# A transformer block's backward pass on one core: where the gate row is multiplied in, and which queues carry the last stores and loads

## The chip, the cores and the metric

The kernel runs on one core of a Trainium2 chip. A core has a matrix engine (TensorE, PE in the profile), an elementwise engine (VectorE, DVE), an activation engine (ScalarE, ACT), a general engine (GpSimd, POOL) and a synchronisation engine (SyncE, SP). Each runs its own list of instructions strictly in order and waits on semaphores for the others. Here SyncE, GpSimd and, in a few places, ScalarE also issue the transfers between the chip's memory and the core's on-chip memory. The metric is the device time of one execution in microseconds (us), lower is better.

## The reference, cut to what matters

The program computes the output of one block and all gradients of it.

```python
def _A_ref(x, w_r, w_i):                       # spectral filter over sequence and channels
    X = rfft2(x.astype(float32)) * (w_r + 1j * w_i)
    return irfft2(X, s=(S, D)).astype(bfloat16)
def _B_ref(x, w1, b1, w2, b2):                 # feed-forward with squared relu
    r = relu(x @ w1 + b1)
    return (r * r) @ w2 + b2
mod = (silu(c) @ w_mod)                        # six rows: sa, ca, ga, sb, cb, gb
h = layernorm(x) * (1 + ca) + sa
x = x + ga * _A_ref(h, A_w_r, A_w_i)
h = layernorm(x) * (1 + cb) + sb
x = x + gb * _B_ref(h, w1, b1, w2, b2)
```

S is 2048, D is 512, the hidden size F is 1792, everything in bf16. The gradients asked for are those of x, w_r, w_i, w1, b1, w2, b2, c and w_mod. Two matter here. With g the incoming gradient and h = r*r the hidden rows, w2's gradient is the product of h transposed with (g * gb), and b2's is the column sum of g * gb. Since gb is one row, the same for every token, it can be multiplied into the product after it is formed or into g before.

## The kernel before

The 2048 rows are held as 16 tiles t of 128 partitions by 512 channels (`NT` = 16). Instructions are traced by a Python program in one order, and a scheduler then places them in each engine's list by priority and by which data and buffers are free; `tc.issue_after(ins)` makes what the block traces come behind `ins` on that engine, and `high_priority` moves an instruction forward. Buffers come from pools with a fixed number of slots per name; a new pool may lie over the memory of a released one, and its first writers then wait for the last users there, stores included.

The program runs forward and backward through the feed-forward part up to about 285 us. What follows is the part that the diff touches.

*The filter phase* (`spec_f23` with `ew_b` and `after_b`, eight groups gi). TensorE transforms a group into PSUM, ScalarE copies it to `G`, VectorE multiplies it with the filter (giving `Z`) and with the saved spectrum (giving the filter's gradient `gW`, three buffers). Each `gW` is stored to out_2 and out_3 by four transfers of 64.2 KB (six of them for gi = 0) on SyncE's queue (L1170). Units of w1's gradient (`grad_w1`, L1126: 16 matmuls, a ScalarE copy, and after every second unit a store on GpSimd's queue) fill TensorE between groups. The modulation gradients (`gm.emit`, with tiles `wmc`, `gmbc`, `gwm` in the pool `gmp`) are put between groups too. At gi = 4 the first two tiles `hn` of the transposed hidden rows are loaded (`load_hn`, a transposing transfer of 512 KB on SyncE's queue); at gi = 5 `gmp` is released and g is loaded whole, 2 MB, into `g_sb` in its place.

*The G1 phase* (`spec_g1`, eight groups). TensorE multiplies `Z` into PSUM (`psG`, four buffers); VectorE (L351) and ScalarE (L353) copy alternate halves to `CS`. Every later `psT` needs the whole of `CS`.

*The row phase* works on eight pairs of tiles. For each pair: TensorE forms `psT` (L375), ScalarE copies it to `Tsb` (L377), TensorE forms `psY` (L385), ScalarE copies it to `gs` (L1276). VectorE unfolds it to `gh1` (L266 to L270) and multiplies by a row, giving `gn` (L1278); ScalarE scales it and sums it (L1280); VectorE multiplies `gh1` with the loaded rows `n1` (`q1`, L1281) and sums a product (`jk1`, L1285), scales the two sums (L1287), applies them to `n1` (L1289, one instruction for each tile of the pair), adds (L1290), adds the loaded `gxl` (L1292), and SyncE stores the result (L1293). `load_rows3(t + 4)` then loads `n1` and `gxl` for the pair after next, from a pool `fin` with two buffers. TensorE also adds up columns (`colsums1`, L1262), two pairs behind.

Between the pairs `fill` puts units of w2's gradient, 14 in all: `grad_w2(fc)` is 16 matmuls of `hn` with `g_sb` (L1203) into one of two PSUM buffers `mm`, then one instruction that takes it out, and the store (L1207):

```python
        with tc.high_priority():
            nc.vector.tensor_tensor(gw, ps, modb[:, GB_B, :], op=ALU.mult)
        nc.sync.dma_start(out6_view[:, fc, :], gw)
        load_hn()
```

`modb[:, GB_B, :]` is the gate row gb on all partitions. `hn` has two buffers in `hnp`, two in `gwp` and four in `endp`; the last pool exists once the w1 units are done. `grad_b2` sums g's columns on TensorE and multiplies the row by gb at the end (`add_quadrants` with `scale`, L1107). The last two modulation gradients (j = 0 and 1, L456 to L477) and the last units of w2's gradient close the program.

Of the kernel before, what the change touches and what calls it, by code (L numbers as in the profile page):

```python
# [18 lines left out]
D = 512  # L19
DF = 257  # L20
# [314 lines left out]

def spec_g1(tc, K, Z, CS):
    nc = tc.nc
    with tc.tile_pool(name="psG", bufs=4, space=PSUM) as psG_pool, tc.tile_pool(name="psF", bufs=1, space=PSUM) as psF_pool:
        psF = psF_pool.tile([P, 4, P], FP32, name="psF")
        for gi in range(8):  # L340
            for hh in range(2):
                n = 2 * gi + hh
                ps = psG_pool.tile([P, 2, 2 * P], FP32, name="psG")
                for ch in range(2):
                    for ri in range(2):
                        nc.tensor.matmul(ps[:, ch, :], lhsT=Z[gi][:, hh, ri, ch:256:2],  # L346
                                         rhs=K["LG"][:, n, ri:ri + 2, :].rearrange("p y m -> p (y m)"), start=(ri == 0), stop=(ri == 1))
# [96 lines left out]
class GMod:  # L444
# [12 lines left out]

    def emit(self, jc, q, row, pool, ppool):

# [21 lines left out]
def kernel(  # L481
# [586 lines left out]

    lf2 = tc.alloc_tile_pool(name="lf2", bufs=1, side="right")
    gmp = tc.alloc_tile_pool(name="gmp", bufs=1, side="right")  # L1070
    K["LF"] += [lf2.tile([P, 2, 3, P], BF16, name=f"LFb{gi}") for gi in range(4, 8)]
# [20 lines left out]

    def add_quadrants(ps, pool, out, scale=None):
        w = ps.shape[-1]
# [5 lines left out]
        def add():  # L1100
# [13 lines left out]
    def run_later(n=1):  # L1114
        if later:
            later[0][0] -= n
            if later[0][0] <= 0:
                later.pop(0)[1]()

    w1o = {}  # L1120
# [28 lines left out]
    with tc.tile_pool(name="f23b", bufs=2) as fr, tc.tile_pool(name="ewb", bufs=2) as ew:  # L1149
# [14 lines left out]
        def ew_b(gi, G):  # L1164
# [3 lines left out]
            for i, o in enumerate((out_2, out_3)):  # L1168
                for p0_, n, rows_ in w_parts(o, gi):
                    K["gW"] = nc.sync.dma_start(rows_, gW[p0_:p0_ + n, i, :, 0:DF]).ins  # L1170

        def after_b(gi):
            if gi + 4 < 8:
                load(gi + 4)
            if gi == 3:
                with tc.issue_after(K["gW"]):
                    nc.sync.dma_start(K["LG"], LG_dram)
            fill_w1(2 if 0 < gi < 6 else 1)
            if gi == 4:
# [9 lines left out]
            if gi in (0, 1, 3, 4):  # L1189
                gms.pop(0)[1]()  # L1190
                if len(gms) > 1:
                    gm.load(gms[1][0], gmp)
# [3 lines left out]
    fin = tc.alloc_tile_pool(name="fin", bufs=2, side="right")  # L1196
    gwp = tc.alloc_tile_pool(name="gwp", bufs=1, side="right")
    endp["gw"] = gwp

    def grad_w2(fc):  # L1200
# [4 lines left out]
        with tc.high_priority():  # L1205
            nc.vector.tensor_tensor(gw, ps, modb[:, GB_B, :], op=ALU.mult)  # L1206
        nc.sync.dma_start(out6_view[:, fc, :], gw)  # L1207
        load_hn()

    def grad_b2():  # L1210
        ps = psX.tile([P, D], FP32, name="mm")
        for t in range(NT):
            q = 32 * (t % 4)
            nc.tensor.matmul(ps[q:q + 32, :], lhsT=K["ones_q"], rhs=g_sb[:, t, :], start=(t < 4), stop=(t >= 12), tile_position=(0, q))
        add_quadrants(ps, gwp, out_7[None, :], modb[0:1, GB_B, :])

    rows3 = {}

    def load_rows3(t):
        if t < NT:  # L1220
            rows3[t] = (fin.tile([P, 2, D], BF16, name="n1"), fin.tile([P, 2, D], BF16, name="gxl"))
            nc.sync.dma_start(rows3[t][0], n1_dram[:, t:t + 2, :])
            nc.sync.dma_start(rows3[t][1], gx1_dram[:, t:t + 2, :])

    with tc.issue_after(K["g_load"]):
        load_rows3(0)
        load_rows3(2)
    for _ in range(2):
        load_hn()

    CS = utcs.tile([P, NT, 4, 16, 8], BF16, name="utcs")
    spec_g1(tc, K, Z, CS)
    sp.release()
    lg2.release()
    fp = tc.alloc_tile_pool(name="fin2", bufs=2, side="right")
    psX = tc.alloc_tile_pool(name="psX", bufs=1, space=PSUM)
    units2 = [lambda fc=fc: grad_w2(fc) for fc in range(NFC)]

    def fill(n):
        for _ in range(n):  # L1240
            if units:
                fill_w1(1)
                if not units:
                    gwa.release()
                    gap.release()
                    endp["hn"] = endp["gm"] = tc.alloc_tile_pool(name="endp", bufs=2)
                    endp["more"] = 4
            elif units2:
                units2.pop(0)()
                run_later()  # L1250
                if endp.get("more", 0) > 0:
                    endp["more"] -= 1
                    load_hn()

    with tc.tile_pool(name="psE", bufs=2, space=PSUM) as psE, tc.tile_pool(name="psS1", bufs=1, space=PSUM) as psS1:
# [11 lines left out]
        def row_pair(t, Ts):  # L1267
# [20 lines left out]
            for i in range(2):  # L1288
                nc.vector.tensor_scalar(gn[:, i, :], n1[:, i, :], rr[:, i, 3:4], rr[:, i, 2:3], op0=ALU.mult, op1=ALU.add)  # L1289
            nc.vector.tensor_tensor(gs, gn, gs, op=ALU.add)  # L1290
            gx = fp.tile([P, 2, D], BF16, name="gx")
            nc.vector.tensor_tensor(gx, gs, gxl, op=ALU.add)  # L1292
            nc.sync.dma_start(out1_view[:, t:t + 2, :], gx)  # L1293
            load_rows3(t + 4)

        Ts = g2_pair(0)
        for t in range(0, NT, 2):
# [4 lines left out]
            if t == 10:  # L1302
                grad_b2()
        fill(1)
        late.flush()
        acc1_odd = fp.tile([64, D], FP32, name="acc1_odd", bufs=1)
        nc.scalar.copy(out=acc1_odd, in_=acc1[64:128, :])
        acc1_sb = fp.tile([64, D], BF16, name="acc1_sb", bufs=1)
# [19 lines left out]
    fp.release()  # L1328
    gwp.release()
    fin.release()  # L1330
    endp["g"].release()
    lf2.release()
# [39 lines left out]
```

## Time and profile before

Six runs have a median of 429.61 us (428.13 to 430.58). The profiled execution took 429.44 us; its span, from the first instruction to the last, is 427.7 us, and 1.7 us lie around it.

| Stretch of the span | What runs | us |
|---|---|---|
| 287 to 338 | filter phase and w1's gradient | 51 |
| 338 to 347 | G1 phase | 9 |
| 347 to 356 | first rows, last w1 units | 9 |
| 356 to 412 | row phase with w2 units | 56 |
| 412 to 422.5 | last three w2 units | 10.5 |
| 422.5 to 427.7 | last stores and closing | 5 |

Some groups of that part, as the profile names them: mean ns of one instruction.

| Line | Engine | What | Count | Mean ns |
|---|---|---|---|---|
| L1203 | TensorE | w2 unit matmul, 128x512 | 224 | 388 |
| L1206 | VectorE | gw from PSUM times gb, 128x512 | 14 | 685 |
| L1289 | VectorE | sums applied to n1, 128x512 | 16 | 408 |
| L1290 | VectorE | add, 128x1024 | 8 | 684 |
| L1280 | ScalarE | scale and sum, 128x512 | 16 | 720 |
| L940 | ScalarE | Identity with scale and bias, 128x512 | 16 | 809 |
| L465 | ScalarE | copy from PSUM, 128x512 | 6 | 586 |
| L1170 | SyncE queue | gW store, 64.2 KB, to landing | 30 | 7600 |
| L477 | GpSimd queue | modulation gradient store, 256 KB, to landing | 12 | 6700 |

How to read this: a matmul's duration spans its way through the array, so matmuls that follow each other overlap; 48 of them in a row took 10.48 us, 0.218 us each. Instructions of the other engines overlap a little at their ends: two L1289 in a row took 0.73 us. "Idle before, released by" means that the engine stood still and which event ended it; a stretch's busy time over its length tells which engine is full there.

### The profile page before, as it was taken

The numbers are of one execution on the slowest core, as the hardware profiler recorded it, in microseconds if no ns is written. First come the engines' busy times: TensorE is split into PE (matmuls) and PEld (weight loads), VectorE is DVE, ScalarE is ACT, GpSimd is POOL, SyncE is SP. The second block draws the span as 40 slices with busy tenths as digits, with TensorE's granted clock in tenths as the row PEclk, the third lists the DMA queues.
The fourth block names the chain that finished last, engine by engine and source line by source line (L and its number), as shares of the span: only waits on it lengthen the run. The fifth ranks groups of instructions, "written<-read, shape, count | busy, mean of one in ns | idle before, by whom it ended". The sixth has DMA issues, their size and how long they took to land.

```text
span 427.7 us, 7138 instructions
## 1 busy us (share of the span) xinstructions
PE 398.3 (93%) x2375; PEld 195.6 (46%) x2375; DVE 354.5 (83%) x862; ACT 256.3 (60%) x487; POOL 55.0 (13%) x135
## 2 busy tenths in 40 slices
PE   2789999999899999999999999999999999898995
PEld 0344446654444444444444444455555654343332
DVE  6889868959996488978897998937997956999994
ACT  5578699778882188248634856464756464636331
POOL 7447940000000000000000000002221000000011
PEclk9999999999999999999999999999999999999899
DMA  8999899979497369768975998989899999999983
GB/s 237 243 258 282 239 275 300 315 236 184 147 357 234 121 94 334 208 171 158 320 176 168 181 315 271 277 200 316 270 275 298 191 234 194 211 296 276 248 237 112
DMA packets 144227, 101.11 MB, mean 236 GB/s; under 512 B 98969, under 2 KB 127518, under 8 KB 143806
## 3 DMA queue, kind: packets, MB, share of 16 engines
q1 hardware_dynamic: 141034, 93.03, 83.3%
q0 software_dynamic: 2592, 7.09, 5.4%
q10 hardware_dynamic: 564, 0.53, 0.4%
q8 instruction: 19, 0.31, 0.3%
q14 instruction: 18, 0.15, 0.1%
HBM read 35.44 MB, written 41.60 MB: 180 GB/s over the span
## 4 chain that ended last, share of the span: by engine, by line
PE 53%; DVE 21%; ACT 16%; issue 4%; DMA 2%; POOL 2%; SPq 0%; ACTq 0%; DVEq 0%
PE og L906 12%; PE mm L877 10%; PE mm L1126 10%; PE mm L712 5%; PE mm L1203 3%; PE psG L346 3%; ACT gab L717 2%; PE psC L311 2%; ACT AE L329 1%; DVE jk L1285 1%; ACT Xs L313 1%; ACT AE L330 1%; PE acc L774 1%; DVE l_st L817 1%; PE psB L323 1%
## 5 line engine op out<-in xcount | busy, mean ns | idle before, releaser
L712 PE MATMUL mm<-gT,w2T 128*128 128x512 bf16 x224 | 57.7, 383 | 3.1 <-ACT gab L717 3.1
L877 PE MATMUL mm<-h2T,w 128*128 128x512 bf16 x224 | 53.4, 379 | 1.3 <-ACT r L879 1.2
L1203 PE MATMUL mm<-g_sb,hn 128*128 128x512 bf16 x224 | 52.3, 388 | 2.0 <-DVE gw L1206 2.0
L906 PE MATMUL og<-w1T,gab 128*128 128x512 bf16 x224 | 50.9, 379 | 0.8 <-DVE o L971 0.8
L1126 PE MATMUL mm<-gab,h_sb 128*128 128x448 bf16 x256 | 50.7, 352 | 0.0
L906 PE MATMUL og<-w,h 128*128 128x512 bf16 x224 | 50.1, 379 | 0.0
L879 ACT ACTIVATE r<-mm,b1col 128x512 bf16<-128x512 f32 x56 | 37.0, 686 | 6.1 <-PE mm L877 3.3
L1203 PEld LDWEIGHTS <-hn 128*128 128x128 bf16 x224 | 21.6, 99 | 29.5 <-issue 7.0
L877 PEld LDWEIGHTS <-w 128*128 128x128 bf16 x224 | 21.1, 97 | 30.0 <-issue 8.3
L1126 PEld LDWEIGHTS <-h_sb 128*128 128x128 bf16 x256 | 24.6, 98 | 21.8 <-issue 0.6
L906 PEld LDWEIGHTS <-h 128*128 128x128 bf16 x224 | 21.8, 98 | 26.1 <-issue 1.0
L906 PEld LDWEIGHTS <-gab 128*128 128x128 bf16 x224 | 21.6, 98 | 25.9 <-issue 1.4
L712 PEld LDWEIGHTS <-w2T 128*128 128x128 bf16 x224 | 21.2, 98 | 22.6 <-issue 6.6
L1280 ACT ACTIVATE gs<-gn,inv 128x512 bf16<-128x512 bf16 x16 | 11.4, 715 | 24.5 <-DVE gn L1278 24.5
L919 ACT CAST G<-og 128x512 bf16<-128x512 f32 x16 | 9.2, 581 | 28.1 <-PE og L906 28.1
L295 POOL MEMSET AE<- 128x2 bf16 x4 | 0.3, 102 | 194.1 <-PE mm L877 194.1
L477 POOL DMA_DIRECT2D out_dram<-gwm x12 | 8.7, 730 | 117.4 <-DVE gx L1292 57.2
L881 DVE TENSOR_TENSOR h<-r 128x1024 bf16<-128x1024 bf16 x28 | 19.3, 689 | 4.8 <-ACT r L879 4.8
L717 ACT CAST gab<-mm 128x512 bf16<-128x512 f32 x36 | 21.4, 601 | 1.7 <-PE mm L712 1.5
L475 DVE SCALAR_TENSOR_TENSOR gm_junk<-wmc,onef,gmbc 128x512 bf16<-128x512 bf16 x24 | 18.0, 749 | 3.3 <-ACT gmbc L465 1.5
L715 DVE CAST gab<-mm 128x512 bf16<-128x512 f32 x20 | 13.8, 688 | 7.0 <-PE mm L712 6.7
L377 ACT ACTIVATE Tsb<-psT 128x512 bf16<-128x512 f32 x32 | 18.5, 607 | 1.5 <-PE psT L375 1.0
(290 smaller groups left out, 801.2 us busy)
## 6 DMA issues: line engine op xcount, KB each, us to landing
h_dram<-h SPq DMA_DIRECT2D x28, 256.0 KB, 3.2
gh_dram<-gab SPq DMA_DIRECT2D x28, 256.0 KB, 4.3
w<-in_B_w_dram SPq DMA_DIRECT2D x2, 1792.0 KB
wmc<-in_w_mod_dram SPq DMA_DIRECT2D x12, 256.0 KB, 4.7
out_dram<-gwm POOLq DMA_DIRECT2D x12, 256.0 KB, 6.7
wz_dram<-Z SPq DMA_DIRECT2D x8, 258.0 KB, 4.0
xs_dram<-Xs SPq DMA_DIRECT2D x8, 258.0 KB, 4.4
Z<-wz_dram SPq DMA_DIRECT2D x8, 258.0 KB, 5.7
```

The lines of the kernel that those rows point to most:

```text
L346: nc.tensor.matmul(ps[:, ch, :], lhsT=Z[gi][:, hh, ri, ch:256:2], rhs=K["LG"][:, n, ri:ri + 2, :].rearrange("p y m -> p (y m)"), start=(ri ...
L377: nc.scalar.activation(Tsb, ps, AF.Copy, scale=EF_S)
L475: nc.vector.scalar_tensor_tensor(out=junk, in0=wmc[:, i, :], scalar=K["onef"], in1=gmbc, op0=ALU.mult, op1=ALU.mult, accum_out=self.gsc[:, ...
L712: nc.tensor.matmul(ps, lhsT=w2T[:, dc, fc * P:(fc + 1) * P], rhs=gT[b][:, :, dc, :], start=(dc == 0), stop=(dc == 3))
L715: nc.vector.tensor_copy(out=gaT[b][:, fc, :], in_=ps)
L717: nc.scalar.copy(out=gaT[b][:, fc, :], in_=ps)
L877: nc.tensor.matmul(ps, lhsT=w1[:, dc, (fc + i) * P:(fc + i + 1) * P], rhs=h2T[b][:, :, dc, :], start=(dc == 0), stop=(dc == 3))
L879: nc.scalar.activation(r[:, i, :], ps, AF.Relu, bias=b1col[:, fc + i:fc + i + 1])
L881: nc.vector.tensor_tensor(h2, r, r, op=ALU.mult)
L906: nc.tensor.matmul(ps, lhsT=lhs(fc), rhs=rhs[:, fc, :], start=(fc == 0), stop=(fc == NFC - 1))
L1126: nc.tensor.matmul(ps[:, 0:W4], lhsT=h2_sb[:, t, dc * P:(dc + 1) * P], rhs=ghn[t // 4][:, t % 4, fs], start=(t == 0), stop=(t == NT - 1))
L1203: nc.tensor.matmul(ps, lhsT=hns[fc][:, t, :], rhs=g_sb[:, t, :], start=(t == 0), stop=(t == NT - 1))
```

## The change

- In the G1 phase, after groups 4 to 7, VectorE multiplies a quarter of `g_sb` by gb in place (`scale_g`), behind that group's copy. `grad_w2` then takes its product out with a plain ScalarE copy, and `add_quadrants` no longer multiplies its row.
- In the row phase L1289's two instructions become ScalarE activations (Identity, with scale and bias per partition).
- The `gW` stores of groups 5 to 7 go to GpSimd's queue.
- `gmp` is released at gi = 4 instead of 5, and g is loaded by four transfers instead of one, followed on SyncE's queue by the first `hn` loads; four of these are issued before the row phase's own. The number kept ahead follows the unit's index.
- The first two pairs' `n1` and `gxl` are loaded behind the gW stores of group 3; there are three buffer sets instead of two, and a pair loads for the third one after it.
- The last modulation gradients' `wmc` loads are issued behind the last row loads, and `gwm` has four buffers there.

```diff
-def spec_g1(tc, K, Z, CS):
+def spec_g1(tc, K, Z, CS, after=None):
...
-                    nc.vector.tensor_copy(out=dst, in_=src)
+                    K["cast"] = nc.vector.tensor_copy(out=dst, in_=src).ins
...
+            if after:
+                after(gi)
...
-            gwm = pool.tile([P, 2, D], BF16, name="gwm", bufs=2)
+            gwm = pool.tile([P, 2, D], BF16, name="gwm", bufs=nbuf)
...
-            if scale is not None:
-                nc.vector.tensor_tensor(row, row, scale, op=ALU.mult)
...
+    def load_rows3(t):
+        if t < NT:
+            pool, n = (endp["fp"], 1) if t % 6 == 4 else (fin, 2)
+            rows3[t] = [pool.tile([P, 2, D], BF16, name=x, bufs=n) for x in ("n1", "gxl")]
+            nc.sync.dma_start(rows3[t][0], n1_dram[:, t:t + 2, :])
+            K["rows"] = nc.sync.dma_start(rows3[t][1], gx1_dram[:, t:t + 2, :]).ins
...
-                    K["gW"] = nc.sync.dma_start(rows_, gW[p0_:p0_ + n, i, :, 0:DF]).ins
+                    if gi < 5:
+                        K["gW"] = nc.sync.dma_start(rows_, gW[p0_:p0_ + n, i, :, 0:DF]).ins
+                    else:
+                        nc.gpsimd.dma_start(rows_, gW[p0_:p0_ + n, i, :, 0:DF])
...
                     nc.sync.dma_start(K["LG"], LG_dram)
+                    load_rows3(0)
+                    load_rows3(2)
...
             if gi == 4:
-                with tc.issue_after(K["gW"]):
-                    load_hn()
-                    load_hn()
-            if gi == 5:
                 gmp.release()
...
                 with tc.issue_after(K["gW"]):
-                    K["g_load"] = nc.sync.dma_start(endp["g_sb"], g_view).ins
+                    for t in range(0, NT, 4):
+                        K["g_load"] = nc.sync.dma_start(endp["g_sb"][:, t:t + 4, :], g_view[:, t:t + 4, :]).ins
+                with tc.issue_after(K["g_load"]):
+                    load_hn()
+                    load_hn()
...
-            nc.vector.tensor_tensor(gw, ps, modb[:, GB_B, :], op=ALU.mult)
+            nc.scalar.copy(out=gw, in_=ps)
         nc.sync.dma_start(out6_view[:, fc, :], gw)
-        load_hn()
+        while len(hns) < min(NFC, max(fc + 4, min(2 * fc + 6, 8))):
+            load_hn()
...
-    spec_g1(tc, K, Z, CS)
+
+    def scale_g(gi):
+        if gi >= 4:
+            gs = g_sb[:, 4 * gi - 16:4 * gi - 12, :]
+            with tc.issue_after(K["cast"]):
+                nc.vector.tensor_tensor(gs, gs, modb[:, GB_B, None, :].broadcast_to([P, 4, D]), op=ALU.mult)
+
+    spec_g1(tc, K, Z, CS, scale_g)
...
+    endp["fp"] = fp
+    load_rows3(4)
...
-                nc.vector.tensor_scalar(gn[:, i, :], n1[:, i, :], rr[:, i, 3:4], rr[:, i, 2:3], op0=ALU.mult, op1=ALU.add)
+                nc.scalar.activation(gn[:, i, :], n1[:, i, :], AF.Identity, scale=rr[:, i, 3:4], bias=rr[:, i, 2:3])
...
-            load_rows3(t + 4)
+            load_rows3(t + 6)
...
                 grad_b2()
+                with tc.issue_after(K["rows"]):
+                    gm.load(0, endp["gm"])
+                    gm.load(1, endp["gm"])
...
-            gm.load(j, endp["gm"])
-            gm.emit(j, 32 * j, acc1_sb[32 * j:32 * j + 1, :], endp["gm"], psX)
+            gm.emit(j, 32 * j, acc1_sb[32 * j:32 * j + 1, :], endp["gm"], psX, 4)
```

In the built program the instruction lists differ from group 4 of the filter phase on SyncE's and GpSimd's queues, and from the G1 phase on the other engines. VectorE has 27 instructions less, ScalarE 30 more, counted in the built lists. Before the first `psT` TensorE's list now has 31 matmuls of w1's gradient where it had 14; the ones after it are fewer by as many.

More of the change, by code (lines that the diff above doesn't have):

```diff
@@ L456, in load, with emit @@
             self.tc.nc.sync.dma_start(self.tiles[jc][dc // 2], self.wm_view[:, dc:dc + 2, cs])
-    def emit(self, jc, q, row, pool, ppool):
+    def emit(self, jc, q, row, pool, ppool, nbuf=2):
         nc, K = self.tc.nc, self.K
@@ L1069 @@
     lf2 = tc.alloc_tile_pool(name="lf2", bufs=1, side="right")
+    fin = tc.alloc_tile_pool(name="fin", bufs=2, side="right")
     gmp = tc.alloc_tile_pool(name="gmp", bufs=1, side="right")
@@ L1091, in grad_b1, with add_quadrants @@
         nc.gpsimd.dma_start(out_5.rearrange("(q f) -> q f", q=NFB), b4[0:P:32, :])
-    def add_quadrants(ps, pool, out, scale=None):
+    def add_quadrants(ps, pool, out):
         w = ps.shape[-1]
@@ L1118, in run_later @@
                 later.pop(0)[1]()
+    rows3 = {}
+    def load_rows3(t):
[4 more added lines that the diff above has]
+            K["rows"] = nc.sync.dma_start(rows3[t][1], gx1_dram[:, t:t + 2, :]).ins
     w1o = {}
@@ L1177, in after_b @@
                     nc.sync.dma_start(K["LG"], LG_dram)
+                    load_rows3(0)
+                    load_rows3(2)
             fill_w1(2 if 0 < gi < 6 else 1)
+            if gi in (0, 1, 3, 4):
+                gms.pop(0)[1]()
+                if len(gms) > 1:
+                    gm.load(gms[1][0], gmp)
             if gi == 4:
-                with tc.issue_after(K["gW"]):
-                    load_hn()
-                    load_hn()
-            if gi == 5:
                 gmp.release()
@@ L1187, in after_b @@
                 with tc.issue_after(K["gW"]):
-                    K["g_load"] = nc.sync.dma_start(endp["g_sb"], g_view).ins
[L1189 to L1192, printed above, removed]
+                    for t in range(0, NT, 4):
[3 more added lines that the diff above has]
+                    load_hn()
         spec_f23(tc, K, UT, AEs, None, lambda gi: gwa.tile([P, 2, 2, FP], BF16, name="G", bufs=2), ew_b, after_b)
     g_sb = endp["g_sb"]
-    fin = tc.alloc_tile_pool(name="fin", bufs=2, side="right")
     gwp = tc.alloc_tile_pool(name="gwp", bufs=1, side="right")
@@ L1214, in grad_b2 @@
             nc.tensor.matmul(ps[q:q + 32, :], lhsT=K["ones_q"], rhs=g_sb[:, t, :], start=(t < 4), stop=(t >= 12), tile_position=(0, q))
[L1215 to L1227, printed above, removed]
+        add_quadrants(ps, gwp, out_7[None, :])
     for _ in range(2):
@@ L1246, in fill @@
                     endp["hn"] = endp["gm"] = tc.alloc_tile_pool(name="endp", bufs=2)
-                    endp["more"] = 4
             elif units2:
@@ L1250, in fill @@
                 run_later()
-                if endp.get("more", 0) > 0:
-                    endp["more"] -= 1
-                    load_hn()
     with tc.tile_pool(name="psE", bufs=2, space=PSUM) as psE, tc.tile_pool(name="psS1", bufs=1, space=PSUM) as psS1:
@@ L1303 @@
                 grad_b2()
+                with tc.issue_after(K["rows"]):
+                    gm.load(0, endp["gm"])
+                    gm.load(1, endp["gm"])
         fill(1)
         late.flush()
-        acc1_odd = fp.tile([64, D], FP32, name="acc1_odd", bufs=1)
+        acc1_odd = endp["gm"].tile([64, D], FP32, name="acc1_odd", bufs=1)
         nc.scalar.copy(out=acc1_odd, in_=acc1[64:128, :])
-        acc1_sb = fp.tile([64, D], BF16, name="acc1_sb", bufs=1)
+        acc1_sb = endp["gm"].tile([64, D], BF16, name="acc1_sb", bufs=1)
         nc.vector.tensor_tensor(acc1_sb, acc1[0:64, :], acc1_odd, op=ALU.add)
@@ L1329 @@
     gwp.release()
+    endp["g"].release()
     fin.release()
-    endp["g"].release()
     lf2.release()
```

## The prediction

> **What bounds the kernel now.** I read the page's busy line first (TensorE 93%, VectorE 83% of the span), then cut the span into stretches, because the diff touches only the last 100 us. The columns are the stretch, then busy us and instruction count per engine, granted TensorE clock, DMA share, GB/s:
>
> ```profile
> 345.00:357.00 12.00, 11.97 (x79) 6.55 (x78) 3.59 (x8) 7.99 (x18) 1.08 (x2) 1.00 0.96 213
> 357.00:372.00 15.00, 13.70 (x80) 6.27 (x79) 13.98 (x33) 5.42 (x14) 0.00 (x0) 1.00 1.06 195
> 372.00:387.00 15.00, 14.68 (x95) 6.49 (x94) 14.34 (x34) 7.30 (x17) 0.00 (x0) 1.00 1.07 300
> 387.00:400.00 13.00, 11.25 (x54) 4.47 (x53) 12.87 (x33) 6.29 (x16) 0.00 (x0) 0.87 0.99 242
> 400.00:412.00 12.00, 11.29 (x54) 4.12 (x53) 11.82 (x30) 6.92 (x15) 0.00 (x0) 1.00 1.02 243
> 412.00:428.00 16.00, 10.61 (x49) 4.59 (x49) 10.13 (x28) 1.97 (x4) 2.90 (x4) 0.98 0.46 153
> ```
>
> From 357 to 412 VectorE (third busy column) works 13.98+14.34+12.87+11.82 = 53.0 of 55 us, 96%; ScalarE 25.9. TensorE's busy time counts waiting inside its pipeline, so I count its work instead. Third, who waited for whom on TensorE (us in all, times, longest) and its timeline where it lost most:
>
> ```profile
> PE mm L1203 <- DVE gw L1206: 2.0, 3, 1.3
> PE psY L385 <- ACT Tsb L377: 1.6, 1, 1.6
> ...
> PE acc L1262 <- DVE gh L270: 0.3, 1, 0.3
> ```
> ```profile
> 390.38 3.62 PE L1203 MATMUL mm<-g_sb,hn 128*128 128x512 bf16 x16
> 395.64 0.86 PE L385 MATMUL psY<-Tsb,TAT 128*128 128x512 bf16 x2 [1.64 <-ACT Tsb L377]
> ...
> 396.78 5.25 PE L1203 MATMUL mm<-g_sb,hn 128*128 128x512 bf16 x16
> ...
> 411.93 10.53 PE L1203 MATMUL mm<-g_sb,hn 128*128 128x512 bf16 x48
> ```
>
> Each 3.62 us group is one w2 unit. After the 1.64 us wait the same 16 matmuls take 5.25 us; the granted clock there is 0.50 (397 to 399 us). The end is a dense run of three units to 422.5; 5.2 us of stores and closing follow. So TensorE's order sets the end, and VectorE decides how often it pauses before 412.
>
> TensorE's work from the first w2 unit (356.30) to 422.5 (66.2 us), at the pace of dense groups: 224 w2 matmuls at 10.48/48 = 0.218: 48.9; six psY pairs at 0.43: 2.6; five psT groups at 0.46: 2.3; eight colsum quads at 0.33: 2.6; grad_b2 1.0; the rest 1.0. Sum 58.4, so **7.8 us are lost**: 3.9 in waits, 5.25−3.62 = 1.6 in half clock, 2.3 in small hand-overs.
>
> **The change, part by part.**
>
> *gw off VectorE.* 14 tensor_tensors (685 ns, 0.60 when packed) go to ScalarE as copies; nearest row the same shape, `gmbc`, 586 ns. *gn off VectorE.* 16 tensor_scalars (408 ns, a pair 0.65) become ScalarE Identity activations with two per-partition operands; nearest row L940, the same form and shape, 809 ns, a pair about 1.5. In the 55 us stage VectorE loses 11×0.60 + 8×0.65 = 11.8 of 53.0; ScalarE gains 11×0.5 + 8×1.5 = 17.5 on 25.9, giving 43.4. TensorE's own work in that stage is 58.4−10.5 = 47.9. The fullest engine is then TensorE; before it was VectorE.
>
> *Gate row into g.* Four tensor_tensors over 128x2048 enter VectorE's order in the G1 phase, each behind a psG cast. Not in the trace; L1290 (half as long) packs at 0.60, so 1.2 each, 4.8 us (between 1.1 and 1.4). They stand where VectorE waited 1.4 us for psG and then 3.7 us for `gs`. Casts 8×0.6, scales 4.8, psF copies with ScalarE's between 2.1, from 338.06, waits included: to about 350 instead of 346.7. The first psT follows at about 350.6 instead of 347.40. The new order covers it: 31 L1126 matmuls stand before psT where 14 stood, 17×0.189 = 3.2 us. If VectorE is held longer, the later psG tiles wait for its casts; I bound this at 0 to 2 us, take 1.0. grad_b2's one-row multiply (0.41) goes too: cover, TensorE's dense tail.
>
> *Row loads early.* This wait goes:
>
> ```profile
> DVE q L1281 <- DMA n<-n_dram: 4.0, 1, 4.0
> ```
>
> It ended at 356.66. The row chain now starts 3.2 us later, but q1 follows gn at once: 351.99+3.2+0.6 = 355.8, so VectorE starts the rows about 0.9 us earlier; I count nothing. Third buffer sets (t+6 instead of t+4) only deepen this.
>
> *SyncE's queue.* It loses 12 gW stores (0.4 to 0.7 us each, some 7), its four early row loads (1.8) move ahead of gW(4), and g is four issues instead of one. g must wait for the pool of the modulation gradients: their last store left GpSimd at 324.2 and takes 6.7 us (up to 8.8), so g issues at 331 to 333. The single 2 MB load took 339.37 to 348.74, the end of a 4.0 us wait of the queue: 2.3 us per quarter. The quarters land from about 335 to 342, with the 1 MB of row loads ahead perhaps to 346. Scaling needs them at 341.7 to about 347. Behind g come the `hn` transposes (3.5 us each on the queue): hn0 and hn1 done by about 341, needed at 356; hn2 and hn3 wait for gW's memory, then are issued before 355 instead of at 356.22 to 362.7. No matmul waited for hn before; with fc+4 kept ahead I expect none: hn4 can follow the last gw1 store, about 363, and is read after 373. wmc waits for the last row load, about 390; used after 404. Cover of all this is 5 to 15 us of TensorE work; without it each us late is one us.
>
> *gW stores by GpSimd.* Here a rule speaks against the change. Nearest row: GpSimd's w loads of the same 64.2 KB, 594 ns issue, 4.1 us to landing, in a stretch with VectorE 83% busy. By it, 12×0.6 = 7 us; the last gW exists at 338.2 and is out by about 347. The Trainium skill ("SBUF — State Buffer", section "A bandwidth-pool intuition that's wrong") says VectorE's two-port modes lock GpSimd out of writing descriptors, 620 ns becoming 3100. Then eight stores after 334.4 take 25 us, to 359, landing 363; ScalarE's first Tsb, which already waited 0.5 us for these stores, would wait 12 us. I side with the row: VectorE runs two-input multiplies and PSUM casts then, not the copies the page names. The cost is nothing. Queued behind gW on GpSimd are three gw1 stores (0.55 each): the first would follow gW(5) (ready at 328.5) by 331, and was issued at 332.95; the last, at 356.45, opens the pool of hn4, and comes after all gW.
>
> *gwm buffers 2 to 4* lie under the 48-matmul tail: nothing.
>
> **The sum.** The waits (3.9) and the half clock they caused (1.6) go: −5.5; the G1 phase +1.0; hand-overs stay. 429.44−4.5 = 424.9 for the profiled execution; the median lies 0.2 higher: **425.0**. Cross-check: 47.9 us at the 96% that the fullest engine reached before is 49.9 instead of 55.6, −5.7. All 7.8 back would be 421.8.
>
> On the half clock a rule bears again. The skill ("TensorE: Matmul & The Clock Gate", Part 1) ties throttling to an idle window of about 3.4 us; here it fell after 1.64 us of waiting. By the page a leftover wait costs its length; by the row 1.6 more. I take the row: this makes one surviving wait dear.
>
> **Rivals.**
> - *ScalarE becomes the limit.* From psY at 359.75 to psY at 395.64 (35.9 us before) TensorE needs 7 units 24.4 + 6.1 + 1.0 = 31.5; ScalarE five pairs of (gs 1.05, Tsb 1.09, gs·inv 1.53, gn 1.5) = 25.9, 7 gw 3.5, one copy 0.6 = 30.0. Both in order, nearly equal: psY waits for a Tsb queued behind a gn that waits for `rr`, or a gw likewise. About 0.5 us for each of five pairs gives back 2.5: 427.4. Against it: two PSUM buffers for each, and VectorE's 41 us leave room.
> - *Hidden anyway.* One such wait late in the stage halves the clock again (3.2), and hand-overs eat 1: 429.2, no change. For: the worst wait was on ScalarE already.
> - *Slower: late g.* VectorE is in order, so a quarter that is late holds the casts behind it, psG, and everything after. The queue's 8 us of LG and row loads before g, plus GpSimd's stores sharing the DMA engines (share 0.92 to 1.22 there), would do it. It turns the sign when the quarters come some 7 us late: first after 349, 4.5 us of gain and 2.5 of TensorE's cover eaten; at 10 us late, 432.5.
>
> **Chances.** Forecast 0.58 (own range 421.8 to 427), ScalarE 0.18, hidden 0.10, late g 0.14. About 0.3%, 1.3 us, can be told from no change. Faster 0.76, same 0.10, slower 0.14. The range to 431 leaves the later part of late g outside, from 421.2 the improbable full return.
>
> **What would show it.** VectorE near 41 us and ScalarE near 43 in the row stage; no wait for `n_dram`; psY at the last pair without a 1.6 us wait; clock 1.00 throughout; first scaled quarter before 343; the dense 48 ending near 418. Wrong, if VectorE waits for g_sb, if Tsb waits for gW, or if TensorE waits for ScalarE's gw as long as for VectorE's.

## The result, and the profile after

The changed kernel takes 430.94 us (median of 35 executions, 427.44 to 435.05), the kernel before, run beside it, 430.46 us (72 executions). The ratio, which leaves disturbed executions out as the medians do not, is **0.9995, 95% interval 0.9978 to 1.0011**: no change. The forecast was 425.0.

The profiled execution of the changed kernel has a span of 430.3 us. First the cut into the stretches that were shown of before (stretch, busy us and instruction count of TensorE, its weight loads, VectorE, ScalarE, GpSimd, then granted TensorE clock, DMA share, GB/s):

```profile
345.00:357.00 12.00, 12.00 (x94) 7.41 (x94) 9.39 (x13) 4.63 (x8) 2.14 (x4) 0.87 1.11 230
357.00:372.00 15.00, 14.19 (x94) 7.24 (x92) 10.21 (x23) 12.40 (x27) 0.55 (x1) 1.00 0.99 213
372.00:387.00 15.00, 15.00 (x87) 6.98 (x86) 14.04 (x35) 13.86 (x29) 0.00 (x0) 1.00 0.88 248
387.00:400.00 13.00, 13.00 (x89) 5.88 (x88) 9.77 (x23) 9.48 (x21) 0.00 (x0) 1.00 0.96 242
400.00:412.00 12.00, 10.14 (x51) 3.45 (x48) 11.38 (x27) 9.64 (x20) 0.00 (x0) 1.00 1.04 238
412.00:428.00 16.00, 14.82 (x68) 6.31 (x67) 8.56 (x25) 8.00 (x14) 2.91 (x4) 1.00 0.60 178
```

Two things have moved. From 357 to 412 VectorE now works 10.21+14.04+9.77+11.38 = 45.4 us and ScalarE as much, and the clock is 1.00 throughout; before, it was 0.87 from 387 to 400. And the stretch with the low clock is now the first one, ahead of the row phase. There the work is late: the row phase's first w2 unit starts at 364.00, where before it started at 356.30.

The longest of what TensorE waited for from 300 us to the end (us in all, times, longest), and its timeline at the worst place and at the last pair (start, us, line, operation, and in brackets how long it stood idle and what ended that):

```profile
PE psG L346 <- DVE utcs L351: 3.3, 1, 3.3
PE psY L387 <- ACT Tsb L379: 2.2, 2, 1.5
PE acc L1271 <- DVE gh L270: 0.3, 1, 0.3
```
```profile
341.00 0.61 PE L346 MATMUL psG<-LGb,Z 128*128 128x256 bf16 x4
344.92 2.72 PE L346 MATMUL psG<-LGb,Z 128*128 128x256 bf16 x12 [3.30 <-DVE utcs L351]
...
402.23 0.38 PE L387 MATMUL psY<-Tsb,TAT 128*128 128x512 bf16 x1 [1.51 <-ACT Tsb L379]
...
416.14 10.53 PE L1217 MATMUL mm<-g_sb,hn 128*128 128x512 bf16 x48
```

The waits for gw are gone. A new one of 3.30 us stands in the G1 phase, and the 12 matmuls after it take 2.72 us: the clock is 0.60 from 344 to 348. In the kernel before the same place reads:

```profile
338.81 1.47 PE L346 MATMUL psG<-LGb,Z 128*128 128x256 bf16 x12 [0.30 <-DVE utcs L351]
```

VectorE's timeline of the changed kernel at that place says why its cast was late:

```profile
339.89 0.69 DVE L421 TENSOR_TENSOR p<-Xb,G 128x1028 bf16<-128x1028 bf16 x1
343.50 0.43 DVE L422 TENSOR_TENSOR gW<-p 128x514 bf16<-128x514 bf16 x1 [2.91 <-DMA out_dram<-gW]
343.84 0.42 DVE L423 TENSOR_TENSOR gW<-p 128x514 bf16<-128x514 bf16 x1
344.18 1.88 DVE L351 CAST utcs<-psG 128x512 bf16<-128x512 f32 x3
...
349.27 1.22 DVE L1241 TENSOR_TENSOR g_sb<-g_sb,modb 128x2048 bf16<-128x2048 bf16 x1
```

This is the `gW` of group 7. `gW` has three buffers, so it takes the one of group 4 and waits until that group's stores have landed. The casts of `psG` are queued behind it. SyncE's queue shows where those stores were, and its waits what held them:

```profile
320.90 2.84 SPq L1181 DMA_DIRECT2D out_dram<-gW  x4
323.79 0.59 SPq L1190 DMA_DIRECT2D LGb<-LG_dram  x1
324.43 0.43 SPq L1127 DMA_DIRECT2D n<-n_dram  x1
324.90 0.43 SPq L1128 DMA_DIRECT2D gxl<-gx_dram  x1
325.63 0.32 SPq L1127 DMA_DIRECT2D n<-n_dram  x1
330.02 0.32 SPq L1128 DMA_DIRECT2D gxl<-gx_dram  x1
330.44 4.30 SPq L1181 DMA_DIRECT2D out_dram<-gW  x4
336.05 5.92 SPq L1204 DMA_DIRECT2D g_sb<-in_grad_out_dram  x4
```
```profile
SPq L1128 <- DMA out_dram<-gW: 4.0, 1, 4.0
SPq L1204 <- DMA gxl<-gx_dram: 4.0, 1, 4.0
```

The fourth row load stood for 4.0 us behind a store of `gW` with which it shares no data. That store (group 3) is the transfer eight places before it on the queue; likewise the second quarter of g waited 4.0 us for the first `gxl`, eight places before it. Group 4's stores went out from 330.44 on, 6.1 us behind the end of LG's issue; in the profile of before they followed LG by 0.1 us:

```profile
321.81 0.58 SPq L1177 DMA_DIRECT2D LGb<-LG_dram  x1
322.49 3.18 SPq L1170 DMA_DIRECT2D out_dram<-gW  x4
```

The four row loads cost the queue not 1.8 us but 6.

Cut at three landmarks (first psG, first w2 unit, the last 48 matmuls, end of the span), the profiled executions stand so:

| | first psG at | G1 to first w2 unit | w2 units to the last 48 | last 48 to the end |
|---|---|---|---|---|
| before | 335.84 | 20.5 | 55.6 | 15.8 |
| after | 338.95 | 25.1 | 52.1 | 14.2 |

The row phase gained 3.5 us and the end 1.6; the G1 phase gave back 4.6: 3.0 of longer waiting for psG, 1.4 of slower psG matmuls, 0.2 of the rest. Of the 3.1 us by which the first psG is late, 2.7 are there before any changed instruction runs (the first w1 unit starts at 282.18 against 279.50), and over all the kernels below the first psG lies between 335.8 and 339.0 in no order: that is scatter of single executions, and the medians decide.

### The profile page after: what moved, and what is told of

Its sections match the earlier page's. It is cut to its first block, busy times and chain, and to the rows that moved or that the text cites. A ratio compares the mean times of both kernels' runs of the same rounds, so it can differ in the third digit from the quotient of the medians.

```text
span 430.3 us, 7168 instructions
## 1 busy us (share of the span) xinstructions
PE 399.4 (93%) x2375; PEld 196.3 (46%) x2375; DVE 346.2 (80%) x835; ACT 275.1 (64%) x517; POOL 62.1 (14%) x147
## 5 line engine op out<-in xcount | busy, mean ns | idle before, releaser
L1217 PE MATMUL mm<-g_sb,hn 128*128 128x512 bf16 x224 | 50.4, 379 | 0.0
L908 PEld LDWEIGHTS <-h 128*128 128x128 bf16 x224 | 21.8, 98 | 26.1 <-issue 1.0
L908 PEld LDWEIGHTS <-gab 128*128 128x128 bf16 x224 | 21.6, 98 | 25.9 <-issue 1.4
L1140 ACT CAST gw<-mm 128x448 bf16<-128x448 f32 x16 | 8.6, 545 | 19.8 <-PE mm L1136 19.8
```

The costliest lines, as they stand in the source:

```text
L908: nc.tensor.matmul(ps, lhsT=lhs(fc), rhs=rhs[:, fc, :], start=(fc == 0), stop=(fc == NFC - 1))
L1217: nc.tensor.matmul(ps, lhsT=hns[fc][:, t, :], rhs=g_sb[:, t, :], start=(t == 0), stop=(t == NT - 1))
```

## The experiments

Each kernel was timed beside the kernel before on one chip; the ratio is to that.

| Kernel | Median us | before | Ratio | 95% interval | Clock 0.997 or more |
|---|---|---|---|---|---|
| after | 430.94 | 430.46 | 0.9995 | 0.9978 to 1.0011 | 7 of 36 |
| e1 gW of group 7 in place | 428.26 | 429.27 | 0.9974 | 0.9951 to 0.9997 | 5 of 17 |
| e2 row loads behind gW(4) | 426.98 | 429.27 | 0.9939 | 0.9914 to 0.9963 | 15 of 22 |
| e3 gW(4) by GpSimd | 428.24 | 429.39 | 0.9977 | 0.9956 to 0.9998 | 5 of 22 |
| e4 gn on VectorE | 428.41 | 429.27 | 0.9980 | 0.9957 to 1.0003 | 10 of 22 |
| e5 before + early row loads | 429.59 | 429.27 | 1.0004 | 0.9985 to 1.0024 | 15 of 22 |
| e6 e2 + gn on VectorE | 425.41 | 429.39 | 0.9906 | 0.9869 to 0.9942 | 6 of 6 |
| e7 e2 + gw on VectorE | 426.42 | 429.39 | 0.9928 | 0.9891 to 0.9964 | 7 of 7 |
| e8 gW(4) behind g | 428.14 | 429.39 | 0.9963 | 0.9943 to 0.9984 | 8 of 22 |
| e9 e2 + both on VectorE | 429.93 | 429.77 | 1.0006 | 0.9981 to 1.0032 | 11 of 22 |
| e10 e6 again | 426.56 | 429.77 | 0.9932 | 0.9908 to 0.9956 | 17 of 22 |
| e11 e2 again | 427.64 | 429.77 | 0.9951 | 0.9927 to 0.9975 | 13 of 22 |
| e12 row loads behind g, gn on VectorE | 427.13 | 430.78 | 0.9918 | 0.9887 to 0.9948 | 10 of 12 |
| e13 e6 + scaling behind the casts | 426.79 | 430.78 | 0.9893 | 0.9854 to 0.9933 | 5 of 6 |

The last column counts the executions whose mean granted clock was at least 0.997, among all with a recorded clock (36 for the changed kernel, one more than its median counts). The kernel before kept it in 138 of the 190 executions timed beside e1 to e13, on four chips. For the changed kernel's own chip the clock of the kernel before is not recorded.

### gW's buffer and the place of the row loads (e1, e2)

```diff
# e1
-            gW = ew.tile([P, 2, 2, FP], BF16, name="gW", bufs=3)
+            gW = ew.tile([P, 2, 2, FP], BF16, name="gW", bufs=3) if gi < 7 else Xt[gi].rearrange("p y r f -> p r y f")
# e2
                     nc.sync.dma_start(K["LG"], LG_dram)
-                    load_rows3(0)
-                    load_rows3(2)
...
                 with tc.issue_after(K["gW"]):
+                    load_rows3(0)
+                    load_rows3(2)
                     for t in range(0, NT, 4):
```

> The changed kernel, but the gW of group 7 is written over its own spectrum tile, so that VectorE no longer waits for the store of group 4 to give its buffer back; all queues keep their order. Theory (the gain was eaten where VectorE waited 2.9 us for gW's buffer, TensorE then 3.3 us for the psG casts, and the clock fell): that wait and the 3.3 us go, the clock stays at 1.00 from 340 to 352, and the time falls by 4 to 5 us against the changed kernel, to about 426.5, ratio to before about 0.990. Rival (g's quarters are late, or ScalarE is full in the row phase): VectorE meets the next wait a few us later at the scaling, and the time falls by less than 1 us.

> The changed kernel, with the four early row loads issued behind the gW stores of group 4 and ahead of g, instead of ahead of those stores; nothing else. Theory: the stores of group 4 go out about 7 us earlier, the buffer is free when group 7 needs it, TensorE's 3.3 us for psG go: 4 to 5 us less than the changed kernel, about 426.5, the same as the kernel that writes group 7 in place. Rival (the row loads' bytes, not their place, delay everything): no change against the changed kernel, about 430.5.

(In e1 the scheduler also puts the first cast ahead of that gW.) In both profiles VectorE's wait for gW is gone and TensorE waits at most 0.3 us for psG. e2's queue and TensorE's timeline:

```profile
322.01 0.58 SPq L1190 DMA_DIRECT2D LGb<-LG_dram  x1
322.69 3.91 SPq L1181 DMA_DIRECT2D out_dram<-gW  x4
...
333.68 2.00 SPq L1204 DMA_DIRECT2D g_sb<-in_grad_out_dram  x4
```
```profile
340.21 1.47 PE L346 MATMUL psG<-LGb,Z 128*128 128x256 bf16 x12 [0.30 <-DVE utcs L351]
```

The stores follow LG directly, and the issue of g's quarters ends 13.7 us behind LG's start (335.7), where the changed kernel took 18.2 (342.0). From the first psG to the first w2 unit e2 takes 20.6 us, as before. (In e11, the same kernel once more, it took 24.2, with g late; see below.) e2 and e11 are below the changed kernel with intervals that do not touch its own: **the place of four loads on the queue is worth some 2.4 us by e2, 1.9 by e11**. It is not the 4 to 5 that were expected. One likely reason is that the changed kernel's profile was a bad one of its kind: e4, whose code is the same up to the row phase, waited 1.1 us for gW and not 2.9. e1 gains less than e2, 0.9 us by the ratios, and its interval overlaps the changed kernel's; its rival had said so. There the next holder shows: VectorE waits 1.6 us for a quarter of g, and TensorE 2.0 us at the first psT. So late g is a second cost beside gW(7), and in e1 the row loads stand ahead of both.

### The same suspicion from other sides (e3, e5, e8)

```diff
# e3
-                    if gi < 5:
+                    if gi < 4:
# e8: the four stores of gi == 4 are kept back and issued here
                 with tc.issue_after(K["g_load"]):
+                    for o_, g_ in gw4:
+                        K["gW"] = nc.sync.dma_start(o_, g_).ins
                     load_hn()
# e5, in the kernel before; its own load_rows3 calls behind g_load are taken out
                     nc.sync.dma_start(K["LG"], LG_dram)
+                    load_rows3(0)
+                    load_rows3(2)
```

> The changed kernel, with the stores of group 4 on GpSimd's queue too, so that on SyncE's queue the row loads hold up nothing but g. Theory (the place of those stores behind the row loads is the loss): as good as the kernel with the row loads behind them, 2 to 3 us under the changed kernel, ratio to before about 0.993, with TensorE's clock at 1.00 in most runs. Rival (what helped there was that g came no later, or GpSimd's queue is itself slow): no better than 1 us under the changed kernel.

> The kernel before, with only one thing of the change: the four early row loads are issued behind LG and ahead of the gW stores of group 4. Theory: it alone brings the wait for gW's buffer and the psG stall, 3 to 5 us more than before, about 434; the 4.0 us wait for n goes but gains nothing. Rival (the stall in the changed kernel comes from the other moved transfers, g in quarters and the h loads, and the row loads are harmless): within 1 us of before, or up to 1 us less since the wait for n is gone.

> The changed kernel, with the suspected cost made larger: the stores of group 4 are issued behind the four quarters of g too. Theory: they land some 4 us later, VectorE waits as much longer for gW's buffer, TensorE for psG; 3 to 5 us more than the changed kernel, ratio to before about 1.009, the clock below 0.997 in nearly all runs. Rival (the buffer is not what decides): within 1 us of the changed kernel, or faster, since g comes earlier.

In size e3 fits the rival, 0.8 us under the changed kernel by the ratios. Its profile does not show the rival's reason. There is no wait for gW, and although the queue stood 7.9 us for the modulation gradients' stores, g is issued at 334.09 and lands 9.1 us later, much as in e2 (333.68, 9.6); the G1 phase takes 20.6 us. What is longer than in e2 is the row phase, 53.8 us against 51.9, with a fall of the clock that is shown below. In 17 of 22 executions the clock fell; why so much more often than in e2, which has the same wait there, stays open.

e5 is a miss in its size. The mechanism is there: VectorE waits 1.0 us for gW's buffer and TensorE 1.4 us for psG. But the time is that of before. Its G1 phase lost 1.1 us against before (21.6 to the first w2 unit) and its row phase took 54.1 instead of 55.6, with n there early and the clock up. So a wait of a microsecond alone does not make a loss in the time. In the changed kernel the late g can come on top, since only there g is needed in the G1 phase; how much of its loss that makes no run separates.

e8 didn't enlarge the wait. Group 4's stores, issued from 334.44, took 13.3 to 14.4 us to land, but gW(7) was written at 337.98 without waiting for them: it must have taken another buffer. It became another way of taking the wait away, and it is 0.9963, as its rival had it; as a test of a longer wait it says nothing. g was issued ahead of the stores, yet its last quarter took 14.5 us to land, and VectorE waited 1.0 us for it, TensorE 1.2 us at the first psT. The two kernels without the wait for gW whose profiles show g late (e1, e8) lie at 0.9974 and 0.9963, e2 and e11 at 0.9939 and 0.9951; the intervals of e1, e8 and e11 overlap.

### Who had to be unloaded in the row phase (e4, e6, e7, e9)

```diff
# e4 (on the changed kernel), e6 and e9 (on e2): gn
-                nc.scalar.activation(gn[:, i, :], n1[:, i, :], AF.Identity, scale=rr[:, i, 3:4], bias=rr[:, i, 2:3])
+                nc.vector.tensor_scalar(gn[:, i, :], n1[:, i, :], rr[:, i, 3:4], rr[:, i, 2:3], op0=ALU.mult, op1=ALU.add)
# e7 and e9 (on e2): gw
-            nc.scalar.copy(out=gw, in_=ps)
+            nc.vector.tensor_copy(out=gw, in_=ps)
```

> The changed kernel, with gn back on VectorE as tensor_scalar. Theory (the row phase is now set by TensorE, and both other engines have room): VectorE's 4.5 us of waiting for ScalarE's gn go, it gets some 5 us of work back, and the time is the same as the changed kernel's within 1 us, about 430.5. Rival (ScalarE is what holds the row phase back): 1.5 to 2.5 us less, about 428.5. Third possibility (VectorE is still the limit): 1 to 2 us more.

> The row loads behind the stores of group 4, and gn back on VectorE. Theory (in the row phase TensorE sets the time and the place of gn is worth nothing): the same as with the row loads moved alone within 1 us, ratio to before 0.992 to 0.996, VectorE's 4.5 us of waiting for ScalarE's gn gone and nothing gained by that. Rival 1 (ScalarE full): 1 to 2 us less, ratio 0.990. Rival 2 (VectorE still the limit): 1 to 2 us more, ratio 0.998.

> The row loads behind the stores of group 4, and w2's product taken out by VectorE (a plain copy, since g is scaled already) instead of ScalarE. VectorE's work in the row phase rises by some 7 us to about 48 of 52 us. Theory (the row phase's gain came from unloading VectorE): most of it goes again, TensorE waits for gw, 2 to 3 us more than with the row loads moved alone, ratio to before 0.999 to 1.001. Rival (the gain came from n1 and the h loads being there early): within 1 us of the row loads moved alone, ratio 0.993 to 0.996.

> The row loads behind the stores of group 4, and both gn and w2's product back on VectorE, so that ScalarE takes over nothing in the row phase; the scaled g, the early loads and the queues stay as changed. Theory (VectorE's load is what held the row phase back, and taking off either part was enough): VectorE is again at some 53 of 55 us, TensorE waits for gw and psY for 3 to 4 us, ratio to before 0.998 to 1.001. Rival (the early n1 and h loads made the gain, and unloading VectorE none of it): the same as with gn alone on VectorE, ratio 0.990 to 0.993.

e4 can't be told from the changed kernel, and its row phase takes 52.2 us, the changed kernel's 52.1. With both back on VectorE (e9) the whole gain is gone, though g is scaled and all loads are issued as early as in e2. (g landed later in e9's profile, and its G1 phase is 1.2 us longer than e2's; by the ratios e9 is 2.4 to 2.9 us behind e11 and e2.) TensorE's waits are not those expected: 0.5 us for gw, 1.5 us for q, none for psY. But VectorE is full again, as the stretch between e9's first w2 unit and its last ones shows (third busy column 52.63 of 54 us):

```profile
359.00:413.00 54.00, 52.06 (x295) 22.50 (x292) 52.63 (x128) 27.37 (x63) 0.55 (x1) 1.00 0.99 244
```

With either one on ScalarE (e2 has both, e6 gw, e7 gn) the row phase takes 51.4 to 51.9 us from the first w2 unit to the last 48. So the gain is the unloading of VectorE, and one of the two moves was enough for it. e7's expectation had VectorE's load right (about 48 of 52 us; 48.1 of 51.4 were measured, 49.1 of 51.9 in e6) and was wrong that this is too much: VectorE had just enough room.

The second move brings a wait of its own. ScalarE's and TensorE's timelines of e2 at the last pairs:

```profile
393.22 0.61 ACT L379 ACTIVATE Tsb<-psT 128x512 bf16<-128x512 f32 x1
393.71 1.52 ACT L1298 ACTIVATE gn<-n,rr 128x512 bf16<-128x512 bf16 x2
395.12 0.60 ACT L379 ACTIVATE Tsb<-psT 128x512 bf16<-128x512 f32 x1
```
```profile
393.88 0.38 PE L387 MATMUL psY<-Tsb,TAT 128*128 128x512 bf16 x1
395.77 0.38 PE L387 MATMUL psY<-Tsb,TAT 128*128 128x512 bf16 x1 [1.51 <-ACT Tsb L379]
```

The two gn, 1.52 us, stand between the two Tsb of a pair, and the second psY waits 1.51 us for them. That same wait is in the profiles of after, e1, e2, e3, e8 and e11, the kernels with both moves. With gn on VectorE the pair of Tsb stays together; psY there waited 0.4 to 0.8 us, and in e13 1.53 us, behind a ScalarE that had itself waited for VectorE. In e7, with gn but not gw on ScalarE, psY did not wait. But the row phase is not shorter without that wait: e6 takes 51.9 us as e2 does, since TensorE waits 1.41 us for `gh` on VectorE instead. The 1.51 us is the same in all six, but what follows differs. In e2 the clock stayed at 1.00. In e3 it did not (the stretch from 396 to 400, clock third from the end, and the wait in it):

```profile
396.00:400.00 4.00, 3.09 (x10) 0.84 (x10) 3.86 (x8) 3.81 (x9) 0.00 (x0) 0.62 1.09 263
```
```profile
396.91 0.54 PE L387 MATMUL psY<-Tsb,TAT 128*128 128x512 bf16 x1 [1.51 <-ACT Tsb L379]
```

### The rest (e10, e11, e12, e13)

> The kernel with the row loads behind the stores of group 4 and gn on VectorE once more, beside the other two on one chip. Theory (two waits were left in the changed kernel, gW's buffer and a 1.5 us psY wait behind ScalarE's gn, and each of them costs its length and in some executions the clock): no wait over 1.5 us, clock 0.997 or more in nearly all runs, ratio to before 0.989 to 0.992, 1 to 1.5 us under the kernel with the row loads moved alone. Rival (the first measurement was the luck of six runs): ratio 0.994, the same as with the row loads moved alone.

> The kernel with only the row loads moved behind the stores of group 4 once more, for comparison on the same chip. Theory: ratio to before 0.993 to 0.995; the psY wait of 1.5 us is there, and the clock is below 0.997 in a third of the runs. Rival (gn's place is worth nothing): the same ratio as with gn on VectorE.

On one chip the two differ by 0.2% with intervals that overlap: what gn on VectorE brings beyond e2 isn't settled by these pairs (0.9906 against 0.9939, 0.9932 against 0.9951; both point the same way). The profile of e10 shows the holder that is left. VectorE waited for g's quarters, TensorE then for the last of `CS`, and the clock fell (0.57 from 356 to 360):

```profile
347.76 1.23 DVE L1241 TENSOR_TENSOR g_sb<-g_sb,modb 128x2048 bf16<-128x2048 bf16 x1 [2.02 <-DMA g_sb<-in_grad_out_dram]
```
```profile
355.09 0.61 PE L377 MATMUL psT<-Cf,utcs 128*128 128x128 bf16 x8 [2.51 <-ACT utcs L369]
```

g's quarters took 12 us from issue to landing here, in the profile of after 7.6. Two ways to make the kernel deaf to that:

```diff
# e12, with gn on VectorE: the row loads behind g
                 with tc.issue_after(K["g_load"]):
+                    load_rows3(0)
+                    load_rows3(2)
                     load_hn()
# e13, on e6: the scaling behind all of VectorE's copies of the G1 phase (K["cast"] is the last one there)
-    spec_g1(tc, K, Z, CS, scale_g)
+    spec_g1(tc, K, Z, CS)
+    for t in range(0, NT, 4):
+        gs = g_sb[:, t:t + 4, :]
+        with tc.issue_after(K["cast"]):
+            nc.vector.tensor_tensor(gs, gs, modb[:, GB_B, None, :].broadcast_to([P, 4, D]), op=ALU.mult)
```

> gn on VectorE, and the four early row loads behind g's quarters, ahead of the h loads. Theory (g comes late because the row loads stand in front of it on the queue): the quarters issue at about 331 to 334 instead of 334 to 338, VectorE does not wait for g, the clock is 0.997 or more in nearly all runs, ratio to before 0.988 to 0.991. Rival (g waits for the memory of the modulation gradients, whatever stands on SyncE's queue): g issues no earlier, ratio 0.992 to 0.995 as with the row loads ahead of g.

> gn on VectorE, the row loads behind the stores of group 4, and the four multiplications of g behind all of VectorE's casts of the G1 phase, where VectorE then waited 3.7 us for the first gs; so a late quarter holds no cast. Theory (late g costs only because the casts queue behind it): no psT wait over 1 us, the w2 units start when they did, about 20.5 us after the first psG, clock 0.997 or more in nearly all runs, ratio to before 0.988 to 0.991. Rival (the row phase is the remaining limit, or the first rows are now held by the scaling): ratio 0.992 to 0.995, or TensorE waits for g_sb at the first w2 unit.

In e12 g is issued at 332.13, no earlier than in e6 (332.06): the queue stood 5.7 us for the modulation gradients' stores, whose memory g takes, which is the rival's reason. And its last quarter still came after 14.8 us, and VectorE waited 1.4 us for it: the place on the queue is not all of it. In e13 nothing waits for g, and the first w2 unit starts 20.6 us after the first psG. The four multiplications fill the time in which VectorE waited for the first gs, at

```profile
348.95 4.61 DVE L1241 TENSOR_TENSOR g_sb<-g_sb,modb 128x2048 bf16<-128x2048 bf16 x4
```

e13 is the best measured, **0.9893 (0.9854 to 0.9933)**, though on six executions; the intervals of e6, e10 and e12 overlap it, so what the place of the scaling adds to e6 is not settled. e6, e7, e10, e12, e13 and the two runs of e2 are faster than both kernels.

## Why the prediction was wrong

**The step that failed is "SyncE's queue".** It said of the row loads: "its four early row loads (1.8) move ahead of gW(4)", and looked for what they would delay only in g and the hn loads. What stood behind them first was group 4's stores, and on these hangs, through three buffers, gW(7) on VectorE, and through VectorE's order the psG casts. The 1.8 us was issue time alone; the queue's wait for the landing of an earlier transfer made it 6 us. With the loads behind those stores the time falls by 2.4 us (e2) or 1.9 (e11), of the 4.5 that were forecast. In the profiles of e2, e6 and e7 the G1 phase then takes 20.6 us, as before, where the prediction had added 1.0; in those of e9, e11 and e10, where g landed late, it takes 21.8, 24.2 and 25.9.

**The G1 phase, "I bound this at 0 to 2 us, take 1.0",** was therefore +4.6 in the profiled execution, and +1.3 in that of e4. The bound had looked at the length of the scaling on VectorE only, which was right: 1.22 us each against 1.2.

**"The quarters land from about 335 to 342, with the 1 MB of row loads ahead perhaps to 346"** was early. They were issued at 336.05 to 341.5 and landed 7.6 us later, from 343.7 to 349.1; about 3 us of this is the later start of that execution. In the changed kernel's profile the wait for gW covered this; those of e1 and e8 to e12 lay it bare.

**"The waits (3.9) and the half clock they caused (1.6) go: −5.5"** was mis-sized in two terms. The row phase gained 3.5. Of the waits 2.5 us stayed, 2.2 for psY and 0.3 for the column sums. The longest, 1.51, is the rival "ScalarE becomes the limit" in its place, a Tsb behind a gn, though not because ScalarE is full (44.7 of 52.1 us). Taking gn back does not win it: TensorE then waited about as long for VectorE. Every kernel measured kept a wait of 1.4 us or more in the row phase; why one takes the other's place is not shown. And 1.6 us of half clock is not in every execution of before: 138 of 190, on other chips, kept 0.997 or more. The changed kernel, with two waits that can set it off, kept it in 7 of 36. The median of these is 428.97; that of the executions under 0.997, without the four longest, is 430.87. So the term was not won but, as far as the chips can be compared, lost more often.

**"5.2 us of stores and closing follow"** was taken as fixed, and a gain of 1.6 was missed. One would look for it in `gcr`, the closing row, which no longer stands behind VectorE's last gw. e7, where it does again, speaks against that:

```profile
419.30 0.69 DVE L1220 CAST gw<-mm 128x512 bf16<-128x512 f32 x1 [1.65 <-PE mm L1217]
419.90 0.20 DVE L1336 COPY gcr<-mm 4x128 bf16<-4x128 bf16 x1
420.44 0.29 SPq L1337 DMA_DIRECT2D out_dram<-gcr  x1
```

The store goes out 11.7 us behind the start of the last 48 matmuls (408.73), as it did before (423.64 against 411.93), and still the end comes 14.2 us behind that start and not 15.8. What shortened the closing stays open.

**Right were** VectorE's relief (53 to 45 us in the same 55; the forecast of 41 was for the work that stood there before, and the stage now starts later and is denser), the price of gn (1.52 a pair, 1.5 was taken) and about that of gw (0.56 to 0.59, 0.5 was taken), the vanished wait for n, and GpSimd's gW stores at nothing. Group 6's four took 2.34 us from 337.44 on, 0.59 each, while VectorE ran its two-input multiplies without a pause. The 3.1 us that the Trainium skill ("SBUF — State Buffer", section "A bandwidth-pool intuition that's wrong") has for such a store beside a VectorE copy was not seen; no such copy ran there. The slower rival named the right line, VectorE's order with the casts in it, and the wrong holder.

e13, with the row loads behind the stores, the scaling behind the casts and gn left on VectorE, has the ratio 0.9893, which is that of 425.0 to 429.61. That does not confirm the sum. It is another kernel, on six executions, its row phase takes 53.0 us, more than the changed kernel's, and the equal number is in part luck.

## What to carry to other kernels

A load that is moved ahead on a queue costs every transfer behind it, and the first to look at are the stores: each holds a buffer, and the instruction that will want that buffer is a whole rotation later, often on an engine where the critical copies are queued behind it. Count a queue's step by its waits for landings, not by its issue times. A transfer whose landing varies by some microseconds is better awaited behind an engine's urgent work than in the middle of it; e13 shows the wait gone, though not yet a gain in time beyond e6. And when one engine is relieved, move only as much as makes it no longer the limit: moving both gn and gw measured no better here than moving one.

## What was not expected of the hardware

- The clock's answer to a wait did not follow from its length. TensorE's waits of 1.51 us left it at 1.00 in the profiles of after and e2 and brought it to 0.62 in e3; 1.64 (before), 2.12 (e11), 2.51 (e10) and 3.30 us (after) brought it to between 0.50 and 0.62; 1.98 us in e1 and 2.25 us in e5 did not. The Trainium skill ("TensorE: Matmul & The Clock Gate", Part 1) has an idle window of about 3.4 us; every fall here came after less.
- A transfer on SyncE's queue that waits for nothing it reads or writes waits for the one eight places before it: in after for a gW store (4.0 us), in e2 and e6 the fourth row load for LG (1.9 and 2.8 us), eight places back in each order. That it is a count of eight is inferred from these.
- The same quarter of g, 512 KB, took 7.6 us to land in the profile of after, 11.3 to 13.7 in e9, e10 and e13, and between 5.9 and 14.8 in e12.
